# A cheaper exp on VectorE and a new written order in a four-layer attention kernel

## The chip, the cores and the metric

One core of a Trainium2 chip runs the kernel. The core has TensorE (PE, matmuls into PSUM), VectorE (DVE), ScalarE (ACT), GpSimd (POOL) and SyncE (SP, which issues most DMAs). The metric is device time in microseconds; the median over several runs is compared. Beside the times there is a profile of one execution.

## The reference

Four layers follow one another on an input of 2048 rows by 512 columns, two sets of weights taking turns (A, B, A, B). Each layer normalises, makes 32 heads of queries but only one head of keys and values, takes a softmax over all 2048 keys, and adds the projected result to its input:

```python
q = (x @ wq).reshape(B, S, H, Dh).transpose(0, 2, 1, 3)     # H = 32, Dh = 16, S = 2048, D = 512
k = x @ wk
v = x @ wv
scores = jnp.einsum("bhqd,bkd->bhqk", q, k) * (Dh ** -0.5)
p = _softmax(scores, axis=-1)
o = jnp.einsum("bhqk,bkd->bhqd", p, v)
return o.transpose(0, 2, 1, 3).reshape(B, S, H * Dh) @ wo   # x = x + this, of layernorm(x)
```

There are 4 x 32 x 2048 x 2048 scores, each of which needs an exp. The inputs are small enough that the kernel takes no maximum away before it; it checks bounds on the way, and a slow general path is taken only if they fail.

## The kernel before

**Tiles.** The exps are worked in 4096 tiles of 128 partitions by 1024 columns of float32. A tile holds scores of 64 keys by 512 queries for 32 (row, column) places of the array, its two halves from the two halves of TensorE's rows. TensorE is used as eight small arrays of 64 rows by 32 columns: row 0 (partitions 0 to 63) and row 1 (64 to 127), four column groups each. A "half" in what follows is work for one of the two rows; four matmuls, one per column group, go out together.

**Two ways to an exp.** Most tiles go to ScalarE: `score` (line 767) issues eight matmuls into one of two PSUM buffers `st` and then the ScalarE activation (line 777) that writes the tile `pt`. The other tiles, 381 of them, go to VectorE. Their score is made half by half into the PSUM bank `by_v` (`score_v`), `exp_first` (lines 800 to 829) writes a scaled and shifted integer image of the score, one half each (line 809), and six more operations on the whole tile, the "chain", turn it into an exp. The integer image holds the exponent in its upper bits and the fraction in its lower 23: the chain masks out the fraction and makes a number between 1 and 2 of it (`mant`, line 823), masks out the exponent (line 825), and evaluates a polynomial of `mant` by Horner's rule in scalar_tensor_tensor operations (lines 826 to 828), the last of which (line 820) multiplies with the power of two. Up to two chains are open at a time. Tiles for VectorE are taken out of the sequence 24 tiles ahead of need.

**PV.** When a tile `pt` is ready, `pv` multiplies it with the values (64 x 32, float32) and accumulates in the bank `acc0` for row 0 and `acc1` for row 1. The piece is 256 columns wide. If the next PE letter of the order asks for the second piece of the same tile in the same row, both are issued as one piece of 512 columns. A float32 matmul shows in the profile as two matmul instructions.

**Products.** The projections (queries, keys and values, output) go step by step into one PSUM bank, `beside`. Each product is 24 steps, 12 for either row, which accumulate into the same bank. The two rows may not write that bank at the same time. So the code keeps a count of turns: a product step of one row is allowed only after the other row's last one is known to have ended (the assertion in `both`, line 482). It is known once a score has waited for a ScalarE exp whose own score came later than that step, or after `touch` (line 904), a VectorE copy of one column of `beside`: it reads what the product wrote, and the next product step writes it again, so each waits for the one before.

**The written order.** The order of all this work is a string of letters, `ORDER` (from line 56), which was made by a planner outside the kernel; no planner runs here. The loop at the end of `fast_path` goes through it. TensorE and VectorE each take their own letters in this order; a letter of one engine holds up the other only through semaphores. The letters:

- S: one score for ScalarE, both rows, and its exp.
- E or O: a PV half of row 0 or row 1. N: two product halves, M: one, V: a score half for VectorE, W: V and M. The table `STEPS` combines what row 0 and row 1 do: a is E and O together, b is N and O, c is E and N, and so on; l is E alone, m is O alone, p and q are one product half alone in row 0 and row 1, n and o are two, r and s are V alone in row 0 and row 1.
- P: a product step with the whole array. F: transposes and sums of squares with the whole array.
- I: the first VectorE operation on a half for VectorE. 0 and 1: the next operation of the older or newer open chain.
- X: VectorE work beside the exps (norms, clamps, copies, residual additions, weight preparation). G: the evacuation of an `acc` bank. D: a step of the softmax division. Y: `touch`. Q: the load of a query tile.

```python
STEPS = {"S": "SS", "a": "EO", "b": "NO", "c": "EN", "d": "MO", "e": "EM", "f": "VO", "g": "EV",
         "h": "WO", "i": "EW", "j": "VM", "k": "MV", "l": "E-", "m": "-O", "n": "N-", "o": "-N",
         "p": "M-", "q": "-M", "r": "V-", "s": "-V"}
...
    def touch():
        V.tensor_copy(seen_by_v, beside[:, 0:1])
        synced[0] = turn[0]
...
                                                        # in both():
                assert start or old[0] == r or old[1] <= synced[0], (bank, old, turn, synced)
```

Of the kernel before, what the change touches and what calls it, by code (L numbers as in the profile page):

```python
# [49 lines left out]
LEAD = 1013283008.0  # L50
C0, C1, C2, C3 = 37.67991256713867, 23.053848266601562, 12.310662269592285, -0.15703019499778748
# [17 lines left out]
    "bSbISb0b0Sa0sSaaYISa0Sfc1Sc0qSaa1Sc0SccISa0qSaaXSa0SaaXSa0kSbIpSb0hSbIpS0a0Sa0aSiqISa0aSi1qSa0Saa1S0bSaY"
    "aISq0cSc0jSaaISc0SaaXSa0SaaXSr0mISQa0SF0SaaXSXaSPPPSPPGPSGsPISaXX0SaaS1a0Saa1Sa0SaaXSa0aSaXSaaXSa0SaPXSf"  # L70
    "aISl0SaaXSP0PSasXSaaISaXSa0aSXrPSaIaXSPSaaSXsXSaIa0SP0PPSa1Sa0rSaa1S0PPPSa1SPPP0SaaISa0SgaISPP0PSaXSa0aS"
    "hpISb0b0Sa0SgaISc0qSic1Sa0Saa1Sb0pSbpISaaY0SjcISc0qSQaaXSa0Shb1Sb0bSaISlGl0SpbGSb0mSaY0SicISc0qSfa1Sc0Sa"
    "aISc0c0SaSaXaSXXaDSaXXaDSaXXSaDXaXSa0sSaIaSXD0mSaaX1Sf0SaaISXaXSF00SaSaXaDSaXSgXmISaD0SflDSFD0SaaXS0SSIa"
    "XSaXaXD0SF0SXaS0aaSXsaISF0SaaXSa0SaaXSa0ShbIS0pa0SaDaS0kbSbIpSDb0rSalYDSc0SQaa1Sc0SaaISa0a0ScScGqqGSqq0S"
    "aaXSaXSaDXa0SaSaX0aSFXSsDaXISaXa0SXa0SaXX0fScIqSc0qScaDS0aSgaISDb0kSbbISbDpS0b0Sa0aSraISc0cSaXSa0aSaXaS0"
    "fScIcS0qc0Sa0sSaaISb0Shb1Sb0pSa1aS0aScIcS0eSaa0SsaISb0bSaXSa0aSaXrSaIa0Sc0Sc0cSm0SgaISb0pShb1Sa0SaaISQc0"
    "qq0ScSa0aSsaISbGpkGSpp0SaaXSa0SaaISaXSaDa0S0jcISc0qScc1Sj0aSa1Sa0aSb1pSaa0SbSbIbD0SkbSIaaY0SiSaXa0SaaISa"
    "XSaDa0SF0SaXa0SjcSIcq0Sic1Sm0Saa1Sb0pSbbISb0ShbISa0SaaY1Sa0Sic1SaXa0SaScIc0SqcSj0cSaaIS0aShb1S0bSaIaS0bb"
    "0SkbISa0SaaYS1Qgq0SeaXSa0SbaISlGpSl0bGSb0ShbISa0pSha1Sa0SaaY1Sc0SaaISc0cSc0SiaSIc0qSaaXSa0ShbISb0pSk0aIS"
    "a0aSa1Si0cScq1Sc0cSc1SaaY0SapSbIb0SaSaXaXXSrDaISaXXaSDaSXXgmDXSXa0SamXS1aXD0SamISa0SaXrSIaaXS0FSaXSa0aSa"  # L80
    "XrSXaDaS0FSXSDXSXXDSF0SISaXa0SaXsSQaIa0Sa0SF1SaXaS0aSaXaS0arSPGPPGSP0PSPPPISa0SaD0aSsaISa0aSaD1Sa0aSa1Sa"
    "0aSa0SfaISP0PSaaDSa0SaaD0SasSaIaDSa0Sg0aISPP0SaaXSaXSa0aSaX0SaaSXa0rSaaISXFS0faISXl0SaX0aSsXSIaaXX0SrSa1"
    "a0SaS1a0SaaIS0SgaISm0Sf1Sa0aSa1Sa0aSlISa0SsaISa0aSr1SQa0aS1Sa0aSGSGlISa0SgaISaD0Saa1Sa0SaaD1Sf0SaaIS0mSa"
    "0SgaISa0SgaDSm0SaaISDm0SaDaS0jcISc0Scc1Sj0qqSaaY1Sb0Sbb1Sbb0SbSaIaXSa0SicISc0Sic1Sa0qSaIaS0qa0SjaSIaq0Sa"
    "aS1a0ShbS1bp0SbbISb0SaaXSa0sSccISc0Sia1Sa0aScISa0a0SjcSaImY0SQhSa1a0Saa1SbGpSpGppS0pbSaIa0SbSaXaDS0scScI"
    "cS0cSi1cSD0aqSaIaY0Sa0ShbSIb0pSgbDSb0SbaXSaXXaDSaXXSaDaXXSa0SalISaXXSa0aXS0fISaX0aSa1Sa0rSaaXSXl0SFSXa0S"
    "aaISaXaSXa0Sa0Sas0SaaISF0SrSX0SISaXaSXaX0Sa0a0SasSaIa0SFS1aXSa0aSaXSa0aSF0SQaXa0SaSaXa0SajSGqqqGScIc0SaS"
    "a0mSkbISaDa0Sh0SaIa0SkaSIaaD0Skp1Sb0aSl1Sa0aScqISaDa0SjSaYIaSDn0SfaDS0lSa1aS0pSaaISaXsXSaISaXa0SXF0SaaXS"
    "0rSaaXS0aSaX0SaaISaX0SaXXs0SaIa0SSa1a0SrSa1a0SS1aaS0SISa0aSa0sSaaISa0SfaISl0Sa0a0SsSIaa0SQaS1ar0Saa1SGSG"
    "l0SaSaIa0SmSDa0aSsaISa0SaaD1Sr0SaaIS0sSaIa0SS1aaDSr0SaaD0SaSaDS0aaSI0Sa0aSsaISa0Saa1Sr0Saa1S0SaIaS0sSaIa"  # L90
    "S0rSa1aS0aSa1S0aaSIS0agSIm0Saa1Sa0SarS1aa0SSIaa0SsISa0aSr1Sa0aSa1Sa0SaaIS0sSaIaS0QrSa1aS0aSa1SGGSl0lSaIS"
    "a0mSaD0SamS0asSaIaD0SaSfaIS0ls0SaIaS0Sa1aSDa0SarSDa0aSDSa0aSppIpSb0b0SkbSIap0SpaS1ar0Saa1Sc0SccISc0qSiaI"
    "Sc0SaaXSf0Sbb1Sa0aSaISc0c0SiqScIc0SQjaS1a0SaaS1bbGS0bSaaISGns0SaSaYIa0SaSi1aXSa0Sbb1Sa0pSaaISb0ShbISa0pS"
    "h1aS0aSaaY1Sc0qSaIaS0cSicIS0qcSi1aSXa0SabS1bp0SaaISb0ShbISb0SaaY1Sa0jScc1Sc0SccISa0qSaXaSXXaS0aaSXQaXS0a"
    "sSaIaXXSmGSfXXlGSlX0SaaISmX0Sa0aS0aSaXmXSF0SaXSa0aSaXSaXa0SFSXsaISaXaXSaX0rSIF0SaXSa0aSaXSa0aSF0SasXSaIS"
    "aXa0SPPP0Sa0Sa0aSa0SaaS0PPPSa0SPPPSPPPSXaSXaaXSXFXSaXaXSXaXXSabSQbpSaaSaSacGScqGSqjqISaSiaISa0qS0aa0Saq0"
    "SeSaY0aSbp0SbbSaXSQaXaScqSaaSqGqqSGqcScjSaIaYSkbISb0Sb0b0SbpSaXlDSXa0SacS0ccSQcD0SccSaYSabGSbpSaaSpGpSla"
    "SbpSbaXSaXSaaSbhSIbpSkpISQbb0SrDaISaDaY0SaDScGcSDi0qSaImSGqqq0SjaS1aq0SaqSD1aaXSa0SaaISaXa0SFSXasXDSaISa"
    "Da0SjcDScDq0SccS1c0SaaYSIapXS0bbXSbXD0SbbSXak0SaaISa0SaaXS0aSaXrSaIaDSa0SaXDlXSaXSasSaaISlXXSaDaXS0SP0PP"
    "SP1SP0PSPP1S0PPSr1PSP0SSIaXSa0aSaXSa0aSkaISa0pSaa0Sh0pISQa0aSkbISb0Saa1Sb0pSaaY1Sc0Saa0SciGScIqSGqo0SjaS"  # L100
    "aIaXSaDXSa0aShp1Sa0aSaISaD0a0SkaSaIa0ShSa1a0Saa1Sc0SaaISc0qSicISc0SiaDSa0qSaaYDS0bSaIaSDpa0Sb0hSIa0SaaS1"
    "hp0SaaXSa0SaaXSa0SaaISF0SXaa0SkbSIa0Saf1Sc0qSaa1Sc0SaaISa0qSiaISa0Sga1Sb0pSQb1bS0bSaaYIScGc0SfSmGmISqa0S"
    "aaXSgDXSa0aSc1Sa0aScISaD0a0SjcScIq0ScaS1rm0Saa1Sb0SbbISb0pSgaISb0ShaXSaDaXSl0Sac1Sc0qSccISc0qS0aSaa0SkaI"
    "Sa0aSkb1Sb0SbbISb0aXSa0SaaXSa0rSccISa0Sia1Sa0qSaqISc0c0SaSa0jSaaYISb0Sfb1Sb0pSaIaS0pb0SkaSIpQaXSa0aSaXSg"
# [12 lines left out]
    "0a0gSmISa0eSrmXSaXa0SFSaX0SaaISaXS0agXSImXS0aaX0SaSaX0rSaaXXS0Sa1a0SSIa0Sa0SgaISa0Sar1Sa0aSm1Sa0aSISa0aS"
    "Qa0gSmISa0aSrGSGSl0aSaIS0amDS0a0SgaISa0SgaD1Sm0Saa1S0mSaaIS0SafDSaISDa0rSaaDS0cSc1cS0mqScIa0Sm0SgaISb0pS"
# [1239 lines left out]
```

## Time and profile before

| | |
|---|---|
| median of 3 runs | 3478.04 us (3476.9 to 3479.99) |
| span of the profiled execution | 3474.3 us |
| TensorE busy, clock granted | 3387.5 us (98%), 0.998 |
| ScalarE busy | 3433.9 us (99%) |
| VectorE busy | 3305.2 us (95%) |
| GpSimd busy | 167.8 us (5%) |
| DMA moved | 147.56 MB, mean 42 GB/s |

The profile is one execution. "L777" is line 777 of the kernel. A group's row gives line, engine, operation, output and inputs with their shapes, the count, then the busy time in us, the mean of one in ns, and the time that its engine stood idle just before these instructions, with what ended the wait. PE counts matmuls, PEld weight loads. Most PE instructions have L495, since one helper, `both`, issues them; they are told apart by the tiles. A row of the timeline gives start and duration in us and how many instructions were drawn together. A row of the view by stretches gives the stretch, its length, each engine's busy time with the number of instructions that touch the stretch, then the granted clock, the DMA share and GB/s.

### The profile page before, as it was taken

How to read it: one execution, taken by the hardware profiler on the slowest of the kernel's cores; microseconds unless marked ns; L12 is line 12 of the kernel's file. 1: busy time of each engine (PE TensorE's matmuls, PEld its weight loads, DVE VectorE, ACT ScalarE, POOL GpSimd, SP SyncE). 2: the span in 40 equal slices, each digit the busy share in tenths (PEclk: the TensorE clock that was granted, in tenths of full speed). 3: DMA queues.
4: the chain of work that ended last, by engine and by line, in shares of the span. 5: the costliest groups of instructions: out<-in, count | busy, mean ns of one | idle time of the engine just before them, and what ended most of it. 6: DMA issues, size and time to landing. Idle time of an engine off the chain costs nothing.

```text
span 3474.3 us, 202688 instructions
## 1 busy us (share of the span) xinstructions
PE 3387.5 (98%) x96011; PEld 2024.7 (58%) x96011; DVE 3305.2 (95%) x4431; ACT 3433.9 (99%) x3745; POOL 167.8 (5%) x137
## 2 busy tenths in 40 slices
PE   9999999999999999999999999999999999999998
PEld 5566566564556656656455665665546666564554
DVE  4889999999989999999998999999999899999997
ACT  8999999999999999999999999999999999999998
POOL 2001000000000000000000100000000000000000
PEclk9999999999999999999999999999999999999999
DMA  3221111110012111111001211111101121110010
GB/s 102 66 78 39 45 45 36 42 39 25 28 45 69 32 44 47 44 28 46 18 30 54 58 42 34 50 36 34 47 14 44 48 54 37 47 44 25 27 37 21
DMA packets 93811, 147.56 MB, mean 42 GB/s; under 512 B 30056, under 2 KB 47976, under 8 KB 92968
## 3 DMA queue, kind: packets, MB, share of 16 engines
q1 hardware_dynamic: 91400, 133.64, 13.0%
q8 instruction: 752, 12.32, 1.5%
q10 hardware_dynamic: 1568, 0.85, 0.1%
q14 instruction: 91, 0.75, 0.1%
HBM read 90.57 MB, written 34.59 MB: 36 GB/s over the span
## 4 chain that ended last, share of the span: by engine, by line
ACT 44%; PE 42%; DVE 10%; issue 2%; DMA 1%; SPq 0%; POOL 0%; DVEq 0%; ACTq 0%; POOLq 0%
ACT pt L777 44%; PE acc L495 22%; PE st L495 11%; PE beside L495 7%; DVE pt L809 2%; DVE poly L828 1%; PE by_v L495 1%; DVE pt L820 1%; DVE poly L826 1%; DVE poly L827 1%; DVE mant L823 1%; DVE pt L825 1%; PE beside L532 1%; DMA qt<-qs 0%; PE beside L389 0%
## 5 line engine op out<-in xcount | busy, mean ns | idle before, releaser
L777 ACT ACTIVATE pt<-st 128x1024 f32<-128x1024 f32 x3715 | 3419.7, 1078 | 12.7 <-PE st L495 10.7
L495 PE MATMUL acc<-pt,vop 64*32 64x256 f32 (+1 forms) x50536 | 2797.5, 440 | 2.9 <-DVE sum L925 1.2
L495 PE MATMUL st<-qt,kop 64*32 64x512 f16 x29720 | 1685.6, 380 | 68.5 <-ACT pt L777 52.4
L495 PEld LDWEIGHTS <-kop 64*32 64x32 f16 x32768 | 795.6, 90 | 1009.1 <-issue 744.1
L495 PEld LDWEIGHTS acc<-pt,vop 64*32 64x32 f32 x50536 | 1227.6, 106 | 259.0 <-issue 8.1
L809 DVE TENSOR_SCALAR pt<-by_v 128x512 int32<-128x512 f32 x762 | 521.2, 684 | 44.4 <-PE by_v L495 30.8
L828 DVE SCALAR_TENSOR_TENSOR poly<-poly,mant 128x1024 f32<-128x1024 f32 x381 | 467.4, 1227 | 0.7
L820 DVE SCALAR_TENSOR_TENSOR pt<-poly,pt 128x1024 f32<-128x1024 f32 x381 | 466.7, 1225 | 0.6
L827 DVE SCALAR_TENSOR_TENSOR poly<-poly,mant 128x1024 f32<-128x1024 f32 x381 | 464.1, 1218 | 1.8
L826 DVE SCALAR_TENSOR_TENSOR poly<-mant 128x1024 f32<-128x1024 f32 x381 | 464.0, 1218 | 0.0
L495 PE MATMUL beside<-wo,ot 64*32 64x512 f16 x5472 | 402.3, 376 | 0.1
L495 PE MATMUL beside<-xnT,wq 64*32 64x512 f16 x5376 | 390.5, 376 | 0.9 <-DVE gv L432 0.7
L495 PE MATMUL by_v<-qt,kop 64*32 64x512 f16 x3048 | 303.8, 377 | 3.0 <-DMA qt<-qs 1.8
L825 DVE TENSOR_SCALAR pt<-pt 128x1024 int32<-128x1024 int32 x381 | 262.0, 688 | 2.7
L823 DVE TENSOR_SCALAR mant<-pt 128x1024 int32<-128x1024 int32 x381 | 261.3, 686 | 1.8
L495 PEld LDWEIGHTS <-ot 64*32 64x32 f16 x5472 | 165.1, 92 | 43.9 <-issue 4.3
L495 PEld LDWEIGHTS <-wq 64*32 64x32 f16 x5376 | 158.0, 92 | 47.5 <-issue 5.5
L440 POOL TENSOR_TENSOR sq<-qs 128x512 bf16<-128x512 f16 x64 | 100.9, 1576 | 934.4 <-DVE qs L437 934.4
L925 DVE COPY sum<-acc 128x512 f32<-128x512 f32 x126 | 82.5, 682 | 14.4 <-PE acc L495 11.7
L376 POOL TENSOR_TENSOR rstd<-var,nhalf 128x4 f32<-128x4 f32 x15 | 28.8, 1918 | 1235.5 <-DVE var L375 1235.5
L495 PE MATMUL beside<-xnT,wkv 64*32 64x512 f16 x1152 | 84.0, 376 | 0.0
L437 DVE TENSOR_SCALAR qs<-beside 128x512 f16<-128x512 f32 x62 | 42.4, 683 | 18.1 <-PE beside L495 7.3
(125 smaller groups left out, 869.7 us busy)
## 6 DMA issues: line engine op xcount, KB each, us to landing
qt<-qs SPq DMA_DIRECT2D x85, 512.0 KB
qs<-qs SPq DMA_DIRECT2D x127, 128.0 KB
rec<-rs SPq DMA_DIRECT2D x63, 256.0 KB
xs<-xt SPq DMA_DIRECT2D x48, 256.0 KB
xt<-xs SPq DMA_DIRECT2D x48, 256.0 KB
sum<-sum SPq DMA_DIRECT2D x252, 32.0 KB
xt<-in_A_x_dram SPq DMA_DIRECT2D x30, 256.0 KB
out_dram<-xt SPq DMA_DIRECT2D x15, 256.0 KB
```

The source lines that it names most:

```text
L437: V.tensor_scalar(qs[:, 0], ps, BIG, -BIG, ALU.min, ALU.max)
L440: G.tensor_tensor(sq, qs[:, 0], qs[:, 0], ALU.mult)
L495: PE.matmul(o[32 * j:32 * j + 32], w[j][h], x[j][h], start=start, stop=stop, skip_group_check=True, tile_position=(64 * r, 32 * j))
L777: e = A.activation(pts[:, i], st[s], AF.Exp, scale=SCALE / UP / UP).ins
L809: w = V.tensor_scalar(e[:, 512 * r:512 * r + 512], by_v, SCALE / UP / UP * LOG2E * 2.0 ** 23, LEAD, ALU.mult, ALU.add).ins
L820: writer[i] = V.scalar_tensor_tensor(p, poly, C0, p, ALU.add, ALU.mult).ins
L823: lambda: V.tensor_scalar(mant.bitcast(I32), e, 0x7FFFFF, 0x3F800000, ALU.bitwise_and, ALU.bitwise_or),
L825: lambda: V.tensor_scalar(e, e, 0x7F800000, None, ALU.bitwise_and),
L826: lambda: V.scalar_tensor_tensor(poly, mant, C3, mant, ALU.add, ALU.mult),
L827: lambda: V.scalar_tensor_tensor(poly, poly, C2, mant, ALU.add, ALU.mult),
L828: lambda: V.scalar_tensor_tensor(poly, poly, C1, mant, ALU.add, ALU.mult),
L925: V.tensor_copy(sums[pr, odd], acc[odd])
```

## The change

The exp on VectorE is split differently. The mask for the fraction keeps 22 bits and not 23, so that `mant` lies between 1 and 1.5, half an octave; the mask for the upper part keeps the exponent and the top bit of the fraction, and ORs a constant into it. Over the half octave a polynomial of one degree less is used: the chain has five operations after `exp_first`'s and not six, three of them scalar_tensor_tensor and not four.

`ORDER` is replaced as a whole. It has 419 tiles for VectorE and 3677 for ScalarE, where it had 381 and 3715. Everything else in the kernel, `STEPS` and the loop among it, is as it was.

```diff
-LEAD = 1013283008.0
-C0, C1, C2, C3 = 37.67991256713867, 23.053848266601562, 12.310662269592285, -0.15703019499778748
+LEAD = 1030161728.0
+C0, C1, C2 = 7.247527122497559, 6.331161975860596, 0.5959731936454773
+HALVES = 0x1A827A
...
         chains.append(deque([
-            lambda: V.tensor_scalar(mant.bitcast(I32), e, 0x7FFFFF, 0x3F800000, ALU.bitwise_and,
+            lambda: V.tensor_scalar(mant.bitcast(I32), e, 0x3FFFFF, 0x3F800000, ALU.bitwise_and,
                                     ALU.bitwise_or),
-            lambda: V.tensor_scalar(e, e, 0x7F800000, None, ALU.bitwise_and),
-            lambda: V.scalar_tensor_tensor(poly, mant, C3, mant, ALU.add, ALU.mult),
-            lambda: V.scalar_tensor_tensor(poly, poly, C2, mant, ALU.add, ALU.mult),
+            lambda: V.tensor_scalar(e, e, 0x7FC00000, HALVES, ALU.bitwise_and, ALU.bitwise_or),
+            lambda: V.scalar_tensor_tensor(poly, mant, C2, mant, ALU.add, ALU.mult),
             lambda: V.scalar_tensor_tensor(poly, poly, C1, mant, ALU.add, ALU.mult),
             last]))
```

A piece of either order, from where products are dense in the new one (before, then after; the strings do not stand at the same work):

```
IpSDb0rSalYDSc0SQaa1Sc0SaaISa0a0ScScGqqGSqq0SaaXSaXSaDXa0SaSaX0aSFXSsDaXISaXa0S
YqYqlSYqqlSmlmlSXXaXSXlmXFSXXaXXfXSpppImSYqqYpnmSYpppYqmSYppYqmlSqqYpslSYImlml0S
```

The letters that the orders hold:

| letter | S | a | l and m | p and q | I | Y | 0 and 1 | P | F | X | D | G |
|---|---|---|---|---|---|---|---|---|---|---|---|---|
| before | 3715 | 3279 | 210 | 506 | 762 | 105 | 2286 | 144 | 93 | 772 | 315 | 168 |
| after | 3677 | 350 | 7020 | 2289 | 838 | 429 | 2095 | 144 | 93 | 772 | 315 | 168 |

More of the change, by code (lines that the diff above doesn't have):

```diff
@@ new lines @@
+    "QXPPPPPPPPPSPPPSSXXpppYqSoSYppsnYqqqlISqqeYpSYqqrqYppSIdpmS0lmXlSm0aSXa0lSFXSlmlXmSXlmXSlmXXlmSQlmX0SmaS"
+    "XaXlXSGmS0llSrXSGFISXlmXlmSXlmSXFsSXlmlISmXlmSXXF0SXlmS0lmXlmSQ0FSlmXSXlma0SbpS0mppmpSpspppYqSqoIlSYppYo"
+    "qlSqqqrSGImeGeSlSXlXmaXSF0SXlmXlmS0lmSQXXlmXX0lmSlmXS0almSXaSXXalmXGSrmSIlmXlmSGlS0lmlmSXXlmSXslXmIlSm0m"
+    "S0lmlXSmXS0FSQXlmaXSlmXS0FSlmXaXSlmXXSFGsSXalISmXlSGFXSaSXlm0lqqSqeYqSYnpYqqqSYpppYoqSYqrYppmISQppm0nSmX"
+    "aSXalXSF0SXlm0aSrmXlSmXlImSXlXXmXlXSmGmS0lmgSGlSXIlmlmXS1aSX1almXSlm1SQlmlXm0SlmS0mlmlS0mlSlmmGSrmlXSIml"
@@ new lines @@
+    "SXGsllImSX0lmS0lmSXlmlm0SFSXaXSmaXSmXl0SQFSXlmlXmSlmXXS0FSlmXlmXSfSGFISXalXSslqGqSIqlql0qSqql0qSql0mlSql"
+    "qYmp0SpmppSpm0pdSQpmpYpSnYqmlXSmlXmSFXSXlmXlmSXXslXmXXSIlqoYnSppYqoSYpnYoqSYqlqYpSGppmprmSYqYlmSIdlXSllG"
+    "SXml0mpSQ0pmnS0pmpdSd0lSpmlm0pSpmlSYpYoloSrYqlmSYIqlmSYsIlmlSqqe0Sl0maGSmqS0lmlSqGqlSXlmXlmSQ0mnSb0dSppm"
+    "pSYqlYqqlSYpYqqqlSYpYmdSYpYqlmSYqlmrSlmlYmSIseISlm0lmSl0mSGmqSGlqq0lmSaXSQaXlmS0pbSd0bSpmlSYpYqqlqSYqYls"
+    "dSYlImqlSYqqrqlSYpmIlm0Sppm0Slm0aSaGScoSGmlXS0mlSQlmXlm0SFSlmXXlmXSXcSXlqXqlqSXmXlmSXrmXlmSXpppmpSpmpmlS"
@@ L195 @@
+    "SlmSIaS0rmlmSIlS0fa1Slm0lSmlSIa0lsSIms0SlmS1lmS1ma0SlS0lmlmSIlm0SrmlSIlmlm0SflS1ml0SmaSIls0SaIlS1smS0maS"
+    "GlSGmm0SllS0maSlImlSDDf0lSIml0mrSlml1Sm0lSmlmS0lSIlmlS0smSIlm0fSlS1lm0lmSS10lmlmS0mlSmlImSl0mSlS0sSIlm0l"
+    "mSg0mlS0mlmSl0mlSmlS0mSDaIaSDlmDrSmaISl0smlISml0rSmIlS0lsmSlm1S0lmlS1mS0lmlmISlm0SrmlSIlm0lmSS1lm0lmSS0l"
+    "m0lmSlm0SaS0maSlaSlmSaaaa"
 )
```

313 lines of the change are left out of this document (175 added, 138 removed).

## The prediction

> **What bounds the kernel now.** The page comes first: span, engines, clock.
>
> ```profile
> span 3474.3 us, 202688 instructions
> PE 3387.5 (98%) x96011; PEld 2024.7 (58%) x96011; DVE 3305.2 (95%) x4431; ACT 3433.9 (99%) x3745; POOL 167.8 (5%) x137
> PEclk9999999999999999999999999999999999999999
> ```
>
> The span lies 3.7 us under the median of the runs, 3478.04; I sum against the span and add 3.7 at the end. Three engines look full. Next come the groups of instructions with shapes kept apart, which say what each engine is full of.
>
> ```profile
> L777 ACT ACTIVATE pt<-st 128x1024 f32<-128x1024 f32 x3715 | 3419.7, 1078 | 12.7 <-PE st L495 10.7
> L495 PE MATMUL acc<-pt,vop 64*32 64x256 f32 x35536 | 1923.1, 377 | 2.5 <-DVE sum L925 1.2 <-DVE pt L820 0.5 <-issue 0.5
> L495 PE MATMUL st<-qt,kop 64*32 64x512 f16 x29720 | 1685.6, 380 | 68.5 <-ACT pt L777 52.4 <-DVE gv L432 0.7
> L495 PE MATMUL acc<-pt,vop 64*32 64x512 f32 x15000 | 1357.4, 589 | 0.4 <-issue 0.2 <-DVE pt L820 0.2
> L809 DVE TENSOR_SCALAR pt<-by_v 128x512 int32<-128x512 f32 x762 | 521.2, 684 | 44.4 <-PE by_v L495 30.8 <-PE st L495 9.5 <-PE beside L495 1.1
> L828 DVE SCALAR_TENSOR_TENSOR poly<-poly,mant 128x1024 f32<-128x1024 f32 x381 | 467.4, 1227 | 0.7
> L820 DVE SCALAR_TENSOR_TENSOR pt<-poly,pt 128x1024 f32<-128x1024 f32 x381 | 466.7, 1225 | 0.6
> L827 DVE SCALAR_TENSOR_TENSOR poly<-poly,mant 128x1024 f32<-128x1024 f32 x381 | 464.1, 1218 | 1.8
> L826 DVE SCALAR_TENSOR_TENSOR poly<-mant 128x1024 f32<-128x1024 f32 x381 | 464.0, 1218 | 0.0
> L825 DVE TENSOR_SCALAR pt<-pt 128x1024 int32<-128x1024 int32 x381 | 262.0, 688 | 2.7
> L823 DVE TENSOR_SCALAR mant<-pt 128x1024 int32<-128x1024 int32 x381 | 261.3, 686 | 1.8
> ```
>
> ScalarE sets the end: 3715 exps take 3419.7 us and wait 12.7, in all 3432.4, or 0.924 each; the rest of the span, 41.9 us, is start and finish. Its undisturbed step comes from the view by stretches of time, ScalarE alone:
>
> ```profile
> 1445.00:1555.00 110.00, 109.97 (x121) 1.00 0.13 39
> 3330.00:3440.00 110.00, 110.00 (x121) 1.00 0.06 16
> ```
>
> 121 instructions touch 110 us, so 120 steps: 0.917 each. 3715 x 0.917 = 3406.7; the other 25.7 us are late scores.
>
> TensorE looks as full, but that is overlap of its two row halves ("rows" below). What a row really needs comes from the timeline, around one interval with two PV steps (aa):
>
> ```profile
> 1504.18 0.42 PE L495 MATMUL st<-qt,kop 64*32 64x512 f16 x8
> 1504.40 1.06 PE L495 MATMUL acc<-pt,vop 64*32 64x512 f32 x16
> 1505.26 0.42 PE L495 MATMUL st<-qt,kop 64*32 64x512 f16 x8
> ...
> 2648.11 0.42 PE L495 MATMUL acc<-pt,vop 64*32 64x256 f32 x4
> ...
> 2648.35 0.40 PE L495 MATMUL acc<-pt,vop 64*32 64x256 f32 x4
> ...
> 2648.57 0.40 PE L495 MATMUL acc<-pt,vop 64*32 64x256 f32 x4
> ```
>
> A score takes 0.22 of each row, then PV four passes 0.86; score to score is 1.08 for five units, so a unit (512 columns of f16, or one pass of 256 of f32) is 0.215. A pass of 256 columns alone follows the one before it after 0.24 and 0.22 in the last rows. My sums use 0.213 a unit, 1% less than the rows. Adding the units of the written order (S, V and M 1, E, O, N and W 2) gives 13788 a row in both orders, 2941 us, and with whole-array work about 3040: 0.82 us per exp tile, against ScalarE's 0.917. TensorE has room, if nothing makes it stand.
>
> **The change, part by part.** *The shorter chain.* A tile on VectorE costs 2 x 0.684 + 0.686 + 0.688 + 1.218 + 1.218 + 1.227 + 1.225 = 7.63 us now. One scalar_tensor_tensor (1.22) goes; the second tensor_scalar gets an OR beside its AND, which I cost at nothing: L823 with two operations takes 686 ns, L825 with one 688. So 6.41. 381 x 7.63 = 2907 becomes 419 x 6.41 = 2686; VectorE's busy time falls from 3305 by 221 before what follows. It is not the bound, so this by itself moves nothing.
>
> *38 tiles fewer on ScalarE.* 38 x 0.917 = 34.8 us off. TensorE's work is the same: a V half costs a row a unit as a score does.
>
> *The new order.* Counted letter by letter, it is another schedule. Paired PV steps (a) fall from 3279 to 350; lone ones (l, m) rise from 210 to 7020. 512-wide PV pieces fall from 1875 to 295, which turns 1580 long passes a row into 3160 short ones; at 0.22 to 0.24 a pass against 0.215 that is 16 to 79 us of a row in the whole kernel, within TensorE's room of some 330. I take nothing of it, because the 0.22 stands beside passes that were not waiting; the upper end goes into the range. And Y, VectorE's read of bank `beside` (touch, L906), goes from 105 to 429. A Y stands where a product moves from one row to the other: the next product matmul waits for the read, and the read for the product before it.
>
> What a Y costs, from two places of the timeline, the chain around the second, and the groups:
>
> ```profile
> 67.16 0.38 PE L495 MATMUL beside<-xnT,wkv 64*32 64x512 f16 x1
> ...
> 67.59 0.16 DVE L906 COPY seen<-beside 128x1 f32<-128x1 f32 x1 [4.42 <-PE st L495]
> ```
> ```profile
> 2647.58 0.41 PE L495 MATMUL st<-qt,kop 64*32 64x512 f16 x8
> ...
> 2647.90 0.15 DVE L906 COPY seen<-beside 128x1 f32<-128x1 f32 x1
> ...
> 2648.10 0.40 PE L495 MATMUL beside<-wo,ot 64*32 64x512 f16 x4
> ```
> ```profile
> 2646.85 1.13 DVE poly L827
> 2647.98 0.08 DVE seen L906
> 2648.06 0.04 issue
> 2648.10 0.40 PE beside L495 x4
> ```
> ```profile
> L906 DVE COPY seen<-beside 128x1 f32<-128x1 f32 x105 | 15.8, 150 | 11.9 <-PE st L495 6.3 <-PE beside L495 5.4
> ```
>
> At 67 us VectorE was already waiting (4.42 idle), and the read began 0.43 after the last product matmul; it takes 0.15; at 2648 the next product starts 0.05 after it. So product to product 0.63, with VectorE free. At 2648 also: the score holds the rows to 2647.80, then TensorE stands for 0.30, and the PV matmuls of the step behind wait too (2648.11): the queue stops at the product. The read was late because a 1.22 us operation stood before it.
>
> In the old order every Y has a score and at least one PV step between the two products, so the 0.63 is worked away. In the new one, PE work between the two products is: nothing for 139 Ys, one score for 61, one half step for 43, a score and a half for 81, more for 105. Mean standing time over both rows: nothing between, one row idles 0.63 and the other 0.63 - 0.21, mean 0.52, x 139 = 73; one score takes 0.21 from each, 0.31 x 61 = 19; one half step (0.43 of one row) 0.31 x 43 = 13; score and half 0.1 x 81 = 8. Sum 113 us. Following the rows through the whole order letter by letter (0.213 a unit, 0.63 across each Y) lengthens them by 119, from 3043 to 3163.
>
> Over the whole kernel that fits under 3677 x 0.917 = 3372. But the Ys come in clusters: 283 of 429 lie in 13 of 61 stretches of 60 tiles, where the rows need 0.872 a tile without Ys and 0.970 with them. VectorE has almost only Ys there (276 follow another Y directly), so 0.63 is about right. ScalarE cannot make up a late score: it has two score buffers. So I sum what groups of n neighbouring tiles need over 0.917 a tile. On the old order that gives 62, 40, 23 and 6 us for n = 2, 3, 4, 10; the trace's own number is 25.7, so n is 4. On the new order n = 4 gives 126. The lone half steps alone (Y at zero) give 24, no better and no worse than the pairs. Loss by Ys: 126 - 23 = 103 us; bounds 42 (n = 60) and, if a round trip takes 0.8 because VectorE is busy, 185 - 27 = 158.
>
> Sum: 3474.3 - 34.8 + 103 = 3542.5, + 3.7 = **3546**. VectorE: 3305 - 221 + 324 x 0.15 = 3133 busy, far from the bound.
>
> *A rule against the row.* The timeline has this for S, then l behind a (row 0 four PV passes, row 1 two):
>
> ```profile
> 753.53 0.41 PE L495 MATMUL st<-qt,kop 64*32 64x512 f16 x8
> ...
> 753.75 1.04 PE L495 MATMUL acc<-pt,vop 64*32 64x512 f32 x16
> ...
> 754.47 0.54 PE L495 MATMUL st<-qt,kop 64*32 64x512 f16 x8
> ```
>
> Row 0 is taken to 754.60, yet the next score's matmuls begin at 754.47 and last 0.54, not 0.41: row 1's four, issued second, went first. Rows run free of each other, and lone half steps lose nothing. The Trainium skill, page "TensorE: Matmul & The Clock Gate", section "The mechanism", says the contrary: matmuls start and end strictly in program order. Here trace and page differ, and my sum goes by the trace.
>
> **Rivals.** *ScalarE keeps its step* (faster). The rows' standing falls into time that TensorE has anyway, and only the tile count shows: 3474.3 - 34.8 + 3.7 = 3443. For it: 329 us of room over the kernel. Against: where the Ys are, the rows need more than ScalarE's step. It decides from a loss under 34.8, a round trip near 0.4, which is less than 0.43 + 0.15 + 0.05.
> *VectorE late at the Ys* (slower still). With 0.8 a round trip 3474.3 - 34.8 + 158 + 3.7 = 3601, with 1.2, as when a read stands behind one 1.22 us operation, the sum is 342 - 39 = 303 and the time 3746. For it: the row at 2647.98; against: the Ys that follow Ys.
> *Rows in strict order.* A half step would hold the other row's next score. Longest row per step, n = 4: 175 - 19 = 156, 3599. The 754.47 row speaks against it. By the Trainium skill's page "TensorE: Matmul & The Clock Gate" this would be the result.
> *No change*: the clusters even out over some 60 tiles, loss 42: 3474.3 - 34.8 + 42 + 3.7 = 3485.
>
> **How the numbers follow.** Forecast 0.58 (its own range 3500 to 3600), ScalarE's step kept 0.24, VectorE late 0.07, strict order 0.05, no change 0.06. A measurement here tells about 0.2%, 7 us, from nothing. Slower 0.70, same 0.06, faster 0.24. The range reaches to 3440, which leaves half of the faster rival out, and to 3630, which leaves out the worst of the late VectorE.
>
> **What would show it.** Right: L777 x3677 with a mean step of 0.917 in quiet stretches and 0.95 or more in the 13 dense ones; seen L906 x429 in the chain of waits with several per cent; TensorE waiting on L906, which no row shows now; L809, L820 and L823 at today's durations, three scalar_tensor_tensor a tile, VectorE near 3130 busy. Wrong: products following Ys without a gap, or dense stretches at 0.92 a tile; then the faster rival holds. Quiet stretches slower than 0.917 would mean that the lone half steps cost what I put at nothing.

## The result

The changed kernel takes 3655.93 us (3652.48 to 3659.45), the one before 3477.49 beside it: a ratio of 1.0515, 95% interval 1.050 to 1.053. It is slower by 178 us. The forecast was slower, by 68, with a range that ended at 3630: the sign was right, the size was not.

The page of the changed kernel: span, engines, queue q8, the chain of waits, and groups. Queue q8 brings TensorE's instructions: it fetched 851 times here, and TensorE's 217313 instructions make 849 blocks of 256.

```profile
span 3656.9 us, 228536 instructions
PE 3521.8 (96%) x108651; PEld 2254.6 (62%) x108651; DVE 3205.0 (88%) x4640; ACT 3440.1 (94%) x3707; POOL 130.7 (4%) x137
...
q8 instruction: 851, 13.94, 1.6%
...
PE 60%; ACT 25%; DVE 10%; issue 2%; DMA 1%; SPq 0%; POOL 0%; DVEq 0%; POOLq 0%
...
L829 ACT ACTIVATE pt<-st 128x1024 f32<-128x1024 f32 x3677 | 3425.8, 1079 | 190.9 <-PE st L547 174.0
...
L872 DVE SCALAR_TENSOR_TENSOR pt<-poly,pt 128x1024 f32<-128x1024 f32 x419 | 512.3, 1223 | 4.6
...
L875 DVE TENSOR_SCALAR mant<-pt 128x1024 int32<-128x1024 int32 x419 | 288.7, 690 | 11.6
L877 DVE TENSOR_SCALAR pt<-pt 128x1024 int32<-128x1024 int32 x419 | 289.6, 692 | 4.0
L957 DVE COPY seen<-beside 128x1 f32<-128x1 f32 x429 | 67.2, 157 | 254.6 <-PE beside L547 235.7
```

The same rows of the page before:

```profile
q8 instruction: 752, 12.32, 1.5%
...
ACT 44%; PE 42%; DVE 10%; issue 2%; DMA 1%; SPq 0%; POOL 0%; DVEq 0%; ACTq 0%; POOLq 0%
```

The exps on ScalarE (L829) waited 12.7 us before and 190.9 now, 174.0 of it for scores, and the chain of waits has gone over from ScalarE to TensorE. VectorE's operations have their old durations; there are fewer, and VectorE's share of the chain is 10% as before.

The view by stretches, ScalarE alone, each row 60 exps long, three from where Ys are dense and one from a quiet place:

```profile
1099.00:1169.80 70.80, 56.47 (x61) 0.93 0.24 65
...
1977.70:2051.10 73.40, 57.40 (x61) 0.95 0.23 62
2856.40:2924.40 68.00, 57.87 (x62) 1.00 0.17 45
3172.50:3227.50 55.00, 55.00 (x61) 1.00 0.04 14
```

A step is 55.00 / 60 = 0.917 where it is quiet. In the first two rows it is 1.18 and 1.22, but each of them holds one of the long stops shown further down (9.6 and 8.2 us from exp to exp); without it 1.04 and 1.11 are left. The third has 35 Ys and no such stop: 1.13. Call "late" what the distances of neighbouring exps hold above 0.917, summed over the kernel: 22 us before, 239 now. That is 217 more; less the 34.8 of the 38 tiles, 182, which is the difference of the two spans. By their place in the order, the late us are (before, after):

| near a weight preparation | within two tiles of a Y | near the end of a PV group | other steps with products | rest |
|---|---|---|---|---|
| 1, 46 | 3, 157 | 4, 7 | 11, 18 | 3, 11 |

Around a run of Ys the timeline shows TensorE, then VectorE, then ScalarE:

```profile
1090.68 0.40 PE L547 MATMUL beside<-xnT,wq 64*32 64x512 f16 x4
...
1091.34 0.40 PE L547 MATMUL beside<-xnT,wq 64*32 64x512 f16 x4 [0.21 <-DVE seen L957]
1091.35 0.60 PE L547 MATMUL st<-qt,kop 64*32 64x512 f16 x8
1091.99 0.40 PE L547 MATMUL beside<-xnT,wq 64*32 64x512 f16 x4
...
1092.65 0.40 PE L547 MATMUL beside<-xnT,wq 64*32 64x512 f16 x4
```
```profile
1091.12 0.16 DVE L957 COPY seen<-beside 128x1 f32<-128x1 f32 x1 [0.71 <-PE beside L547]
1091.78 0.16 DVE L957 COPY seen<-beside 128x1 f32<-128x1 f32 x1 [0.50 <-PE beside L547]
```
```profile
1090.47 1.02 ACT L829 ACTIVATE pt<-st 128x1024 f32<-128x1024 f32 x1 [0.50 <-PE st L547]
1092.00 1.02 ACT L829 ACTIVATE pt<-st 128x1024 f32<-128x1024 f32 x1 [0.51 <-PE st L547]
```

From product to product it is 0.65 or 0.66 us, and two such turns in one tile make its step 1.53: the round trip has the size that the prediction gave it.

The second place is new. Four times, once in each layer, where VectorE prepares the output weight `wo`, the distance from one exp to the next is 8 to 10 us. SP's queue and VectorE at one of these stops:

```profile
1112.73 1.20 SPq L1007 DMA_DIRECT2D rs<-den  x2
1113.98 2.51 SPq L1010 DMA_DIRECT2D sum<-sum  x4
1116.60 0.66 SPq L1014 DMA_DIRECT2D rec<-rs  x1
1117.31 1.29 SPq L498 DMA_DIRECT2D qs<-qs  x2
1118.64 6.68 SPq L376 DMA_DIRECT2D wst<-in_B_wo_dram  x4
```
```profile
1122.60 0.43 DVE L392 TENSOR_SCALAR wo<-wst 128x512 f16<-128x512 f32 x1 [6.27 <-DMA wst<-in_B_wo_dram]
...
1128.06 1.28 DVE L978 TENSOR_TENSOR sum<-acc,sum 128x512 f32<-128x512 f32 x2
```

The load of the weight stands behind nine DMAs of the division and the queries; VectorE waits 6.27 us for it, with the evacuation of `acc` (L978) behind it in its order, and TensorE's next PV group waits for that. Before, VectorE never waited for a weight. The trace shows one thing more there: within each stop the clock granted to TensorE falls to 0.50, and it stays there for 7 to 14 us, 41 us at the four stops together. Apart from the first 45 us and the last 5 it is full everywhere else, among dense Ys too, so the 0.93 and 0.95 in the rows above are these stops and not the Ys.

### The profile page after: what moved, and what is told of

The parts are those of the page before. It is cut to its first block, busy times and chain, and to the rows that moved or that the text cites. A ratio compares the mean times of both kernels' runs of the same rounds, so it can differ in the third digit from the quotient of the medians.

```text
span 3656.9 us, 228536 instructions
## 1 busy us (share of the span) xinstructions
PE 3521.8 (96%) x108651; PEld 2254.6 (62%) x108651; DVE 3205.0 (88%) x4640; ACT 3440.1 (94%) x3707; POOL 130.7 (4%) x137
## 4 chain that ended last, share of the span: by engine, by line
PE 60%; ACT 25%; DVE 10%; issue 2%; DMA 1%; SPq 0%; POOL 0%; DVEq 0%; POOLq 0%
PE acc L547 29%; ACT pt L829 25%; PE st L547 14%; PE beside L547 13%; PE by_v L547 2%; DVE pt L861 2%; DVE poly L879 1%; DVE pt L872 1%; DVE poly L878 1%; PE beside L584 1%; DVE seen L957 1%; DVE mant L875 1%; PE beside L441 1%; DVE pt L877 1%; DMA wst<-in_A_wo_dram 0%
## 5 line engine op out<-in xcount | busy, mean ns | idle before, releaser
L829 ACT ACTIVATE pt<-st 128x1024 f32<-128x1024 f32 x3677 | 3425.8, 1079 | 190.9 <-PE st L547 174.0
L547 PE MATMUL acc<-pt,vop 64*32 64x256 f32 (+1 forms) x63176 | 2975.1, 386 | 30.4 <-DVE sum L978 20.5
L547 PE MATMUL st<-qt,kop 64*32 64x512 f16 x29416 | 1880.5, 381 | 29.0 <-ACT pt L829 10.4
L547 PEld LDWEIGHTS acc<-pt,vop 64*32 64x32 f32 x63176 | 1576.9, 106 | 365.6 <-issue 30.0
L861 DVE TENSOR_SCALAR pt<-by_v 128x512 int32<-128x512 f32 x838 | 572.8, 684 | 55.3 <-PE by_v L547 44.1
L872 DVE SCALAR_TENSOR_TENSOR pt<-poly,pt 128x1024 f32<-128x1024 f32 x419 | 512.3, 1223 | 4.6
L879 DVE SCALAR_TENSOR_TENSOR poly<-poly,mant 128x1024 f32<-128x1024 f32 x419 | 511.9, 1222 | 3.8
L547 PE MATMUL beside<-xnT,wq 64*32 64x512 f16 x5856 | 479.5, 383 | 36.0 <-DVE seen L957 30.0
L878 DVE SCALAR_TENSOR_TENSOR poly<-mant 128x1024 f32<-128x1024 f32 x419 | 512.1, 1222 | 0.0
L547 PE MATMUL by_v<-qt,kop 64*32 64x512 f16 x3352 | 338.8, 379 | 6.8 <-DVE pt L861 5.2
L957 DVE COPY seen<-beside 128x1 f32<-128x1 f32 x429 | 67.2, 157 | 254.6 <-PE beside L547 235.7
```

The lines of the kernel that those rows point to most:

```text
L547: PE.matmul(o[32 * j:32 * j + 32], w[j][h], x[j][h], start=start, stop=stop, skip_group_check=True, tile_position=(64 * r, 32 * j))
L829: e = A.activation(pts[:, i], st[s], AF.Exp, scale=SCALE / UP / UP).ins
L861: w = V.tensor_scalar(e[:, 512 * r:512 * r + 512], by_v, SCALE / UP / UP * LOG2E * 2.0 ** 23, LEAD, ALU.mult, ALU.add).ins
L872: writer[i] = V.scalar_tensor_tensor(p, poly, C0, p, ALU.add, ALU.mult).ins
L878: lambda: V.scalar_tensor_tensor(poly, mant, C2, mant, ALU.add, ALU.mult),
L879: lambda: V.scalar_tensor_tensor(poly, poly, C1, mant, ALU.add, ALU.mult),
```

## The experiments

| run | time, us | ratio to before, 95% interval |
|---|---|---|
| e1, cubic in the old order | 3471.13 | 0.9985 (0.9976 to 0.9995) |
| e2, before, pairs split | 3520.50 | 1.0123 (1.0106 to 1.0140) |
| e8, before, only short pieces | 3540.94 | 1.0186 (1.0169 to 1.0203) |
| e9, before, pairs split, long pieces | 3475.28 | 1.0000 (0.9990 to 1.0009) |
| e17, e9 with uneven steps | 3558.17 | 1.0234 (1.0216 to 1.0253) |
| e3, after with 287 Ys | 3622.39 | 1.0411 (1.0393 to 1.0428) |
| e6, after with 168 Ys | 3593.73 | 1.0334 (1.0317 to 1.0351) |
| e4, after, weights by GpSimd's queue | 3643.38 | 1.0477 (1.0460 to 1.0495) |
| e10, after, early weights | 3632.06 | 1.0449 (1.0431 to 1.0466) |
| e12, after, long pieces | 3641.03 | 1.0478 (1.0461 to 1.0496) |
| e11, e6 with early weights and long pieces | 3562.23 | 1.0248 (1.0231 to 1.0265) |
| e15, after without turns | 3542.67 | 1.0196 (1.0179 to 1.0213) |
| e16, e11 without turns | 3526.07 | 1.0144 (1.0127 to 1.0161) |
| e18, e15 with long pieces | 3515.39 | 1.0108 (1.0091 to 1.0125) |
| e19, e18 with early weights | 3493.00 | 1.0048 (1.0031 to 1.0065) |
| e13, after, whole product steps | 3973.70 | 1.1433 (1.1414 to 1.1452) |
| e14, e1 with whole product steps | 3961.45 | 1.1398 (1.1379 to 1.1417) |

### The chain by itself

The change's lines in `exp_first`, and the old order without one chain letter for each tile:

```diff
-b0ShbISa0SaaY1Sa0Sic1SaXa0
+b0ShbISa0SaaY1SaSic1SaXa0
```

> The new chain alone: the kernel before with the half-octave cubic, its written order kept but for the one letter of each tile that the dropped operation had (381 tiles on VectorE). If the new order is what costs, VectorE loses 381 x 1.22 = 465 us of work that bounds nothing: the time stays near 3478, 3460 to 3482, the lower end if some of the 25.7 us of late scores came from a late VectorE. If the new chain itself costs (another tensor_scalar form, another rhythm at the shared ports), it is over 3500.

Measured 3471.13, 5 us faster than before. The cubic is harmless and worth almost nothing where it moves no tiles; the loss belongs to the order, which takes 185 us more than e1. This is the fastest of all these kernels, the two compared ones among them.

### Pieces, steps and instructions

Two theories for what the finer steps cost: the lone half steps, or the number of TensorE's instructions. A 512-wide piece is four matmuls less than two of 256, which for float32 is 16 instructions of TensorE less, weight loads counted. e2 splits every pair (both change), e8 keeps the pairs and issues all pieces short (only the instructions change), e9 splits the pairs and puts half steps of a row together (only the steps change). A piece of the orders of before, e2 and e9, and e8's edit in `step`:

```diff
-hb1Sa0SaaISQc0qq0ScSa0aSsaI
+hb1Slm0SlmlmISQc0qq0ScSlm0lmSslmI
+hb1Slm0SllmmISQc0qq0ScSl0lmmSslmI
...
-                    carry[r] = parts[r][0][2] == 0 and STEPS.get(then, "SS")[r] == w
+                    carry[r] = False
```

> The kernel before with each paired PV step a written as l and m: the same work in the same order, but nearly no 512-wide PV pieces and a finer step, as in the new order. My prediction put this at nothing: within 10 us of 3478. If lone half steps or short passes are what the sum missed, it is slower by 50 us or more.

> The kernel before with its own order, but every PV piece of 512 columns issued as two pieces of 256; each paired step stays a paired step. TensorE gets 1875 x 16 = 30000 more instructions (the split pairs added 25856 and 44 us). Theory A, TensorE waits for the fetching of its own instructions once a block of 256 is used up faster than the next one arrives: the time rises as it did with the split pairs, 3515 to 3540, and pauses stand at one place of every block of 256 instructions. Theory B, it was the lone half steps that cost the 44 us: no lone step is added, so 3472 to 3485.

> The kernel before with each paired PV step written as two lone half steps, row 0 then row 1, but with the half steps of one row put next to each other between two scores, so that 1732 of the pieces are 512 wide (1875 before, 259 with the split pairs alone). The instructions of TensorE are those of before but for some 2300. Theory A (instruction fetch): 3473 to 3488. Theory B (lone half steps): 3510 to 3530.

Measured: +44, +65 and 0 us. Lone steps cost nothing here, instructions do. In e8 the timeline of TensorE, the chain of waits there, and ScalarE's timeline:

```profile
1066.87 0.70 PE L495 MATMUL acc<-pt,vop 64*32 64x256 f32 x12
1069.31 0.41 PE L495 MATMUL acc<-pt,vop 64*32 64x256 f32 x2 [1.74 <-issue]
```
```profile
1067.14 0.43 PE acc L495 x10
1067.57 1.74 issue
1069.31 0.40 PE acc L495 x2
```
```profile
1064.47 3.78 ACT L777 ACTIVATE pt<-st 128x1024 f32<-128x1024 f32 x4
1070.19 1.02 ACT L777 ACTIVATE pt<-st 128x1024 f32<-128x1024 f32 x1 [1.94 <-PE st L495]
```

TensorE stands for 1.74 us and waits for nothing that the profile names. Counting its instructions from the start, such pauses stand at one place of every 256 (behind number 192). Starts more than 0.2 us apart at that place, with their sum: before 30, 10.7 us, where other places have up to 15; e2 116, 56.5; e8 159, 79.4; e9 37, 12.0; the changed kernel 54, 31.8. Against the kernel before, e2 and e8 have 46 and 69 us more of them, and took 44 and 65 us longer: nothing is left for the short passes themselves. Queue q8 moves 16 KB at a time, 869 times in e8:

```profile
q8 instruction: 869, 14.24, 1.6%
```

It is 117 more than the 752 before; 117 x 256 = 29952, the instructions that e8 adds. In the pause shown the next fetch began 6.3 us after the one before and landed at 1067.75; TensorE went on 1.6 us later. In the median of e8 a fetch begins 1.05 us after TensorE has entered a block and takes 0.97, and no block was entered less than 1.17 us after its landing: 3.2 us in all. The fastest twentieth of e8's blocks take under 3.5 us, so hardly any slack is left; in the kernel before, the median block takes 4.3. Some fetches also begin late: in 20 blocks of e8 past 0.6 of the block, and these hold 26 of the 79 us. The other DMAs kept the 16 DMA engines 61% busy around these 20, and 12% around the rest; that they delay the fetch fits this, but no run tests it. By the Trainium skill, page "Runtime: NRT & Kernel Launch", section "Instruction fetch mechanics", instructions come in blocks of 256 by the engine's own queue while the block before is worked, and this stays hidden because dispatch is slower than the filling. The blocks agree with the trace; that it stays hidden does not, 79.4 us of pauses in e8 against it.

In the changed kernel's own order, lone half steps of a row put together (a piece of after, then e12):

```diff
-ql0qSml0mlSqlm0SemlSQ0qaSlqmlSmlmS
+ql0qS0mmllSqlm0SemlSQ0qaSqmllSlmmS
```

> The changed kernel with its own order, in which lone half steps of one row are put next to each other where nothing but work of the other row or of other engines stands between them and no score is passed: 1304 PV pieces of 512 columns, not 295, and so 16144 fewer instructions for TensorE (of the 25277 that the change added). Theory, instruction fetch: the pauses at the block boundaries, 32 us in the changed kernel, fall to about those of the kernel before (10), and the time by 20 to 40, to 3616 to 3636. Rival, in the new order the pauses lie in time that the Ys take anyway: 3645 to 3657.

Measured 3641.03, 15 us less, between the 20 expected and the rival. The pauses fell to 7.4 us, so some of them had lain in time that the Ys took anyway; the runs without turns, below, show how much.

### The Ys

A Y is needed only where the next product half of the other row would otherwise be unsafe, and 142 of the 429 are not. e3 leaves these out; e6 gives product halves to other rows, so that 168 suffice (after, e3, e6):

```diff
-mlYqYqlSYqqlSmlmlSXXaXSXlmXFSXXaXXfXSpppImSYqqYpnmSYpppYqmS
+mlYqqlSqqlSmlmlSXXaXSXlmXFSXXaXXfXSpppImSYqqYpnmSYpppYqmS
+YmlqqlSqqlSmlmlSXXaXSXlmXFSXXaXXfXSpppImSpppnmSppppmS
```

> The changed kernel without the 142 Ys that no move of a product from one row to the other needs (287 of 429 stay), nothing else changed. If the round trips through VectorE cost the time: 3656 less 28 (my sum over groups of 4 tiles, 131 to 103 us at a round trip of 0.64) to 45 (if the sum is as much too low here as over the whole kernel), so 3611 to 3628. If the Ys are harmless: 3656 within 5.

> The changed kernel with product half steps given to other rows, so that a product stays in a row for longer, and a Y only where the turn goes to the other row: 168 Ys, not 429. Everything else of the order keeps its place. By the sum over four neighbouring tiles that the prediction uses the loss falls from 131 to 79 us: 3656 - 52 = 3604, range 3592 to 3620. If the Ys that are left out were redundant or hidden, it stays where the run with 287 Ys was, 3622, or above.

Measured: 33.5 us less for 142 Ys and 62 less for 261, 0.24 us for each. The sum over four tiles gave 52 for e6. The whole cost is measured by taking the turns away (the general path is switched off in these runs):

```diff
             w, x = self.prods()[n]
...
-            return "beside", beside, cols(w), [x] * 4, first, last
+            if r:
+                return ("acc", 1), acc[1], cols(zeros), [x] * 4, ("acc", 1) not in wrote, False
+            return "beside", beside, cols(w), [x] * 4, n == 0, n == 3 * NC - 1
```

> The changed kernel without turns of bank beside: row 1's product half steps multiply with a weight of zeros and go to bank acc1, which only row 1 writes, and no Y is left. Left out is so row 1's half of every product (the values come out wrong), but TensorE issues the same matmuls in the same order. By the trace of the changed kernel 157 us of the late scores lie within two tiles of a Y, away from the weight loads; with the rest that intervals with products show (0.02 us each) some 16 of them stay. Theory, the Ys are the loss: 3656 - 141 = 3515, range 3500 to 3535. By the prediction's term, 103 us, 3553. Rival, the loss there is that products crowd and the rows are uneven: 3600 to 3645.

Measured 3542.67, 113 us less. The rival falls, and the prediction's 103 was nearer than the 141 that I read off the late scores around Ys. The trace gives a likely reason why these differ: with the Ys gone TensorE runs faster between its other holds, and the pauses at the instruction blocks grew from 31.8 to 53.6 us. The two partly hide each other, so gains of single mends don't add up to the loss.

### The weight loads

e4 issues the weight loads on GpSimd's queue, `G.dma_start` for `SP.dma_start` in `load_w`. e10 leaves them on SP and issues the first two chunks of each weight as soon as the buffers are free:

```diff
+    def load_next(key, c):
+        then = key if c < 2 else ("wq", key[1] + 1) if key[0] == "wo" else ("wo", key[1])
+        if then[1] < NL:
+            load_w(then, (c + 2) % NC)
...
-                work.add_dve("wl", lambda: (load_w(key, 0), load_w(key, 1)), 0)
+                work.add_dve("wl", lambda: None, 0)
...
-            work.add_dve("w", lambda c=c: (w_lo(key, c), c + 2 < NC and load_w(key, c + 2)), 0)
+            work.add_dve("w", lambda c=c: (w_lo(key, c), load_next(key, c)), 0)
```

> The changed kernel with the weight tiles of load_w issued from GpSimd's queue and not from SP's, nothing else changed. If the four long exp gaps (8 to 10 us each, 31 us in all over the step) come from weight loads queued behind the softmax division's DMAs on SP: 3656 - 31 = 3625, with no exp gap over 5 us and no wait of VectorE for a weight tile. If the transfers themselves are late: 3656 and the same gaps.

> The changed kernel with the first two chunks of each weight loaded as soon as the two buffers are free, behind the last use of the weight before, and not at the layer's boundary. The waits of VectorE for the first chunk were 3.8, 6.3, 5.4 and 3.9 us, 19.4 in all; those for the third stay. Theory: they stand on the path, and the time falls by 19 to 24, to 3632 to 3638. Rival, the gap is taken over by what comes next (the products behind it): 3645 to 3657.

Measured 12.5 and 24 us less. e10 is at its theory; e4 lies between its two expectations, and exps still stop for up to 8.3 us in it. Another queue only takes away what stood ahead of the load; the load is still called too late, and its third chunk waits for a buffer, as GpSimd's own waits at the first of the four places show in e4:

```profile
217.02 1.30 POOL L376 DMA_DIRECT2D wst<-in_A_wo_dram  x2
224.08 0.54 POOL L376 DMA_DIRECT2D wst<-in_A_wo_dram  x1 [5.76 <-DVE wo L398]
```

Called early, the waits for the first chunk go; one for the third stays in e10, a bit later, up to 4.0 us:

```profile
1113.42 0.43 DVE L397 TENSOR_SCALAR wo<-wst 128x512 f16<-128x512 f32 x1 [4.01 <-DMA wst<-in_B_wo_dram]
```

### All together, and what is left

e11 puts the three mends together; e16 takes its turns away too. e18 and e19 do so with the changed kernel's own rows.

> The changed kernel with the three mends together: products in rows that need 168 Ys, the first chunks of the weights loaded early, pieces put together to 512 columns. If the three costs are separate, they add: 3594 (168 Ys) - 24 (weights) - 20 to 40 (pieces) = 3530 to 3550. If they hide each other, 3560 to 3590; if one covered the others, below 3520.

> The kernel with the three mends (3562) with its last 168 Ys taken away in the same way, row 1's half of the products left out of the values. 87 us lie near its Ys. Theory, the Ys: 3562 - 80 = 3482, range 3468 to 3498, which is the time of the kernel before: 34.8 won by 38 tiles, and some 40 lost by what is left of the weight waits and by lone products. Rival, crowded products and uneven rows: 3530 to 3560.

> The changed kernel without turns (row 1's half of the products left out of the values, as before) and with its lone half steps put together to 1304 long pieces; rows are as uneven as in the changed kernel. Theory, pauses for instructions and Ys hide each other: without Ys the pauses (54 us) cost about what they are, so 3543 - 40 = 3503, range 3490 to 3512, where the same long pieces gained 15 with the Ys. Rival, uneven rows hold the rest: 3525 to 3543.

> The same with early weights: theory, 24 less than the run without: 3479, range 3465 to 3490; that is 36 over the 3443 of the tile count alone, of which some 15 belong to bank acc1, which this kernel's products share, and 10 to the weight waits that stay. Rival, uneven rows: 3500 or more.

e11 measured 3562.23, over the 3550 expected: 94 us where the single runs have 62 + 24 + 15 = 101, so these three nearly add. e16 gained only 36 by taking away 168 Ys, where 87 lay near them, and came close to its rival. e18 and e19, with the changed kernel's own rows, came to 3515.39 and 3493.00, 12 and 14 over the theory, 3 over the ends of their ranges, and under the rival. So, in the order of taking away:

| | us |
|---|---|
| the changed kernel | 3656 |
| no turns, no Ys | -113 |
| long pieces (15 with the Ys still there) | -27 |
| early weights | -22 |
| what is left, e19 | 3493 |
| the tile count alone, 3474.3 - 34.8 + 3.7 | 3443 |

The last 50 us are not split by an experiment. In e19's trace 17 of its 74 late us lie at weight preparations and 22 near the ends of PV groups (1 and 6 before); the second may be the runs' own, since their products share a bank with PV. TensorE's clock has little part in it: in e19 it was halved for 10.2 us, not counting the very end, which is 5 us of work. e16 has 33 us more than e19. It does the same work, with the products in other rows, so e6 and e11 may have given back there a part of what they saved in Ys; no run tests that alone.

### Uneven rows

e17 asks what uneven steps cost where nothing else changes. In e9's order a lone half step is moved behind the next score at 656 places:

```diff
-hb1Slm0SllmmISQc0qq0ScSl0lmmSslmI
+hb1Sl0SmllmmISQc0qq0ScSl0lmSmslmI
```

> The kernel before with split pairs but long pieces (3475, no cost), made uneven: at 656 places the last lone half step of one row before a score is moved behind that score, so that a row has one half step less in one step and one more in the next. TensorE's work, products and Ys stay; 52 pieces become short. With rows that run free of each other (sum over four tiles of the longer row's running total) the loss grows by 11 us: 3480 to 3492. With rows in strict order (longest row of every step, four tiles) it grows by 151: 3600 to 3640. In between: rows are free over a part of a half step only, and the new order, in which half of the steps are uneven, pays for it.

Measured 3558.17, 83 us more than e9: far from the 11 of free rows over four tiles, and far from the 151 of strict order. Exps that are late by 0.2 to 0.4 us (215 of them, 14 in e9) stand at the steps that have got a half step more. Four tiles seems too long a look-ahead here: a score may be issued only when one of two buffers is free, so TensorE can't work far ahead in the lighter step and is late in the heavier one. Following the free rows through the order with two score buffers, 0.213 a unit and 0.25 to 0.3 from a score's end to its exp, gives 34 to 54 us more for e17's order than for e9's, by what the whole-array steps are put at. For the changed kernel's order without Ys it gives 3 to 8 more than for the one before, and for e16's order 12 to 14 more than for e19's. That is worked out, not measured; the rest of the 83 is open. It speaks against uneven rows as the cause of the 178 us, as e19 does.

### Whole steps

If turns are dear, a product step with the whole array needs none. e13 does this in the changed kernel with early weights and long pieces, e14 in e1 (a piece of e1, then e14):

```diff
-b0ShbISa0SaaY1SaSic1SaXa0
+mP0SfmPISa0Saa1SaSgPlP1SaXa0
```

> The changed kernel with early weights and 512-wide pieces put together, and with every product step done with the whole array (letter P) in place of two half steps, one in each row, at the place of the second of them: no turn of bank beside, no Y, and some 20000 fewer instructions for TensorE; the sum of TensorE's work is the same. With 168 Ys the run with the three mends took 3562, and 98 us of its late scores lay within two tiles of a Y. Theory, the Ys: that loss goes, 3455 to 3490. Rival, a whole step has to wait until both rows have come to its place, and the rows of this order are uneven within a step: 1500 whole steps at 0.05 to 0.1 us each, partly hidden by TensorE's room, 3500 to 3580.

> The cubic in the old order (3471), with every product step done with the whole array in the same way, and no Y. The old order hid its 105 Ys, so by the theory of the Ys little is to be won: 3455 to 3473. By the rival, whole steps that wait for the later row, 3475 to 3530.

Measured 3973.70 and 3961.45: both theory and rival missed by some 400 us. 1500 steps cost 490 us in e14, 0.33 each beyond the work, the wait for the later row counted in. TensorE around one of them:

```profile
410.74 0.60 PE L501 MATMUL acc<-pt,vop 64*32 64x256 f32 x8
411.27 0.39 PE L538 MATMUL beside<-xnT,wq 128*128 128x512 f16 x1
411.59 0.41 PE L501 MATMUL st<-qt,kop 64*32 64x512 f16 x8
```

The PV half is two passes, 0.43, so the whole step could begin at 411.17 and begins at 411.27; the score behind it begins 0.32 later, not 0.213: 0.2 us at the two changes. The other row had nothing to do for the 0.43, which is lost too. How the 0.33 divides between the two over the whole run isn't measured.

## Why the prediction was right and wrong

The forecast lay 110 us under the measurement. Two steps failed: short passes, put at nothing, cost 27 us in the order of taking away, and the order on SP's queue, for which there was no term, 22. The Ys were 10 too low. 50 are left, and their cause stays open.

**ScalarE sets the end, 0.917 undisturbed.** Right before and in quiet places after. After the change TensorE sets it in the dense ones; it has 60% of the chain, 42% before.

**The chain.** Right: three operations of 1.22 us, the second tensor_scalar at 692 ns with its OR, 690 for the first. By itself it changes nothing to speak of: e1. VectorE's busy time was forecast at 3133 and is 3205. The summed durations of its operations fell by 164, forecast 172; but operations behind a wait don't overlap by the 0.08 us that back-to-back ones share, and the busy time counts shared time once.

**38 tiles, 34.8 us.** It fits: the quiet stretch after the change still runs at 0.917, and the late us balance with 34.8 to 1 us. No run moves the 38 tiles alone.

**Short passes, "I take nothing of it".** This step failed. I looked for the cost in the passes (0.22 against 0.215) and found room for it; it is in the instruction stream, which I had not looked at. The page had the row: 752 fetches before. It is 15 us in the changed kernel, 27 without Ys; short pieces in the old order cost 44 and 65.

**Y, 0.63 a round trip, loss 103 us.** Mechanism right, size nearly: 0.645 from product to product in the median, 113 us by e15. The chance for VectorE late at the Ys was small, and it played a small part: of 365 Ys that held the next product, 40 had VectorE at work just ahead, 1.16 us from product to product, where the other 325 have 0.66. That is 40 x 0.5 = 20 us at most.

**The sum over four tiles** was fitted to the kernel before: n = 4 was taken because its 23 came nearest to 25.7. It was near for the Ys (103 against 113, 52 against 62). It fails where one step is heavy behind a light one: 11 against 83 in e17. So "lone half steps lose nothing" holds where the rows stay even from score to score (e9: 0), and not where they don't.

**A step that is not in the prediction** is the order on SP's queue. I counted D's letters and didn't ask where their DMAs stand against the weight loads: 22 to 24 us.

**The rule that was weighed.** By the Trainium skill's page "TensorE: Matmul & The Clock Gate", section "The mechanism", matmuls start and end strictly in program order. The experiments don't bear it out: e17 costs 83 where the longest row of every step gives 151, and e19 leaves 50 in all where it gives 116 for the changed kernel's order without Ys (144, less 28 for the order before, over four tiles).

**Rivals.** ScalarE's step kept (3443) and no change (3485) fell; strict order (3599) fell by e17 and e19; VectorE late is right in sign alone: 3656 lies between its 3601 and 3746, but its mechanism makes 20 us. The forecast's 3546 + 27 + 22 + 10 (Ys) + 50 (left) = 3655 is the account, and it has one open line, the largest.

## What to carry to other kernels

When a written order is cut finer, count the engine's instructions before you cost the cut at nothing, and compare the time that 256 of them take with the 3.2 us that a block's fetch took here, from the entry into one block to the entry into the next. A transfer between two users of one bank costs its round trip only where nothing else stands between: look at how many follow each other, and at what one step can give to the next with the buffers there are. And ask of each moved step which DMAs it issues and what stands behind them on that queue: a cheaper operation gained 5 us here, and with the order made to use it the kernel lost 178.

## What was not expected of the hardware

TensorE can outrun its own instructions: in e8, 159 pauses of over 0.2 us, 79.4 us in all, each at the same place of a block of 256, up to 2.8 us long, and 1.3 to 1.6 us from the landing of the late block to the next matmul in the longest ones. A step of the whole array put in place of two half steps among matmuls of 64 rows cost 0.33 us beyond its work (e14), the wait for the later row counted in. At the four stops of 8 to 10 us TensorE's granted clock was halved for 7 to 14 us (after), and among dense Ys, with their short holds, it was 1.00.
